# Attention backward on one Trainium2 core: fp32 transposes of X in two pairs inside the bank of transposed E, and six of E's transposes moved to DMA

## Chip, core and metric

The kernel runs on one core of one Trainium2 chip. The metric is the device time of one execution in microseconds. Three runs of the kernel before took 2244.68, 2246.61 and 2248.53 us; their median is 2246.61 us.

## What is computed

The reference is a forward pass and its gradients for a gated block over x of 2048 rows by 512 columns: `x + s * g`, where s is attention of the normalised x (32 heads of 16 columns) and g a gate made by an MLP of width 1792. Cut to what matters here:

```python
def _A_ref(x, wqkv, wo):
    qkv = (x @ wqkv).reshape(B, S, 3, H, Dh) ...
    scores = jnp.einsum("bhqd,bhkd->bhqk", q, k) * (Dh ** -0.5)
    p = _softmax(scores, axis=-1)
    o = jnp.einsum("bhqk,bhkd->bhqd", p, v)
    return o ... @ wo
...
_out, _vjp = jax.vjp(_f, A_x, A_wqkv, A_wo, B_w1, B_b1, B_w2, B_b2)
_grads = _vjp(grad_out)
```

The change lies in the attention, where output, dQ, dK and dV of each head are made.

## The kernel before, in words

The program has three parts: a preparation (layer norms, projections, MLP forward, gate), the attention core (function `attention_core`, from about 222 to about 1890 us of the span) and the remaining gradients. Only the attention core is touched.

**Blocks and steps.** The attention runs over 64 blocks: 16 pairs of heads times 4 groups of 512 queries. A block has 16 units, one for each 128 keys, kb = 0 to 15. The loop variable is the step g; unit g belongs to block g // 16 and has kb = g % 16. Below, "step 2" is the step with g % 16 = 2, and "unit 7" the unit with kb = 7. The work of the units is software-pipelined by hand, and the order on every engine is that in which the loop body issues it (no scheduler reorders it). In step g:

- TensorE (PE) makes `d` of unit g (dO times V, L1104, one bank of 512 columns for each of the two heads), the scores `s` of unit g + 1 (L1082), the transposes `tT` of unit g - 1 (L1166), three groups of products of unit g - 1 that are added into the block's bank `X` (L1196, L1199, L1203), and four products `Z` (L1280) of the block 20 steps back.
- ScalarE (ACT) takes the exponential of unit g + 1 into the ring `ets` (L1091), and then copies transposed blocks of unit g - 1 from PSUM to the tile `ek` in SBUF (L1178).
- VectorE (DVE) multiplies `d` by E for both heads of unit g into `gts` (L1121). Between the two it copies the share of the transposed blocks that ACT does not take (list `VCOPY`: 0, 1 or 2 of 7). Further copies come in single steps: `xs` from X in step 0 (L1212), `xt` from XT and a reciprocal in step 2 (L1234, L1244), and the sum `acc` from Z in steps 3 and 11 (L1292, L1294).
- SyncE's queue (SP) issues DMA transposes: `gk` from `gts`, 16 blocks of 128 by 128, after each odd unit (L1137); and `ekd` from `ets`, the one block in eight of E that TensorE does not transpose, 4 or 8 blocks at a time, in steps 4, 6, 12 or 14 (L1147, L1151, L1153).
- GpSimd (POOL) computes small factors from `xt` after step 2 and issues loads for the next pair of heads.

**The ring of E.** `ets` has three slots of four units. Unit kb of chunk c (four units a chunk) writes the quarter kb % 4 of slot c % 3, so the exponential of units 12 to 15 overwrites what units 0 to 3 of the same block left. An exponential waits for every reader of what it overwrites, DMA transposes included.

**PSUM.** Eight banks: two for `s`, one for `tT` (seven blocks of 128 by 128 in bf16), three that rotate among the `d`, one for X, one for Z. In step 2 of the next block, four fp32 transposes of `xs` (`XT`, L1222) take one of the three rotating banks; DVE copies it whole to `xt`, and the factors of the softmax and dQ and O follow from it.

Of the kernel before, what the change touches and what calls it, by code (L numbers as in the profile page):

```python
# [8 lines left out]
bf16 = mybir.dt.bfloat16  # L9
f32 = mybir.dt.float32  # L10
ACT = mybir.ActivationFunctionType
ALU = mybir.AluOpType
# [1005 lines left out]
def attention_core(ctx, ctx_r, tc, k, grads, Oall, dQall, dKVT_out, ident_f32, ident_bf, npairs=16, nqc=4):  # L1018
    nc = tc.nc
# [3 lines left out]
    ps_t = ctx.enter_context(tc.tile_pool(name="ps_t", bufs=1, space=PSUM, reuse_waits="tile"))  # L1023
    ps_d = ctx.enter_context(tc.tile_pool(name="ps_d", bufs=3, space=PSUM, reuse_waits="tile"))
# [8 lines left out]
    xsp = sb("xsp", 1)  # L1033
    finp = sb("finp", 1)
# [6 lines left out]
    ets = etp.tile([128, 3, 4, 2, 4, 128], bf16, name="ets")  # L1041
# [44 lines left out]
    def emit_exp(g):  # L1086

        a = a_unit(g)
        if a is None:
            return  # L1090
        nc.scalar.activation(out=st_et[g][:, :, :, a[1] % 4, :].rearrange("k b h q -> k h b q"),  # L1091
                             in_=cur["s"][:].rearrange("k h (b q) -> k h b q", b=4), func=ACT.Exp)
# [17 lines left out]
    def emit_mult(g):  # L1110
        a = a_unit(g)
        if a is None:
            emit_cT(g - 1, 7 - VCOPY[(g - 1) % 16], 7, nc.vector.tensor_copy)
            return
        kb = a[1]
        if kb % 2 == 0:
            cur["gts"] = gtp.tile([128, 2, 2, 512], bf16, name="gts")
        gts = cur["gts"]
        st_gt[g] = gts
        for hj in range(2):  # L1120
            nc.vector.tensor_tensor(out=gts[:, kb % 2, hj, :].rearrange("k (b q) -> k b q", b=4),  # L1121
                                    in0=st_d.pop((g, hj))[:].rearrange("k (b q) -> k b q", b=4),
                                    in1=st_et[g][:, :, hj, kb % 4, :], op=ALU.mult)
            if hj == 0:
                emit_cT(g - 1, 7 - VCOPY[(g - 1) % 16], 7, nc.vector.tensor_copy)

    def emit_dmat(g):
        a = a_unit(g)
# [19 lines left out]
        if kb % 8 == 6:  # L1148
# [3 lines left out]
            else:  # L1152
                nc.sync.dma_start_transpose(out=ek[:].rearrange("q c a k -> q (c a) k"),  # L1153
                                            in_=ets[:].rearrange("k s b h a q -> k (s b h) (a q)")[:, 8 * sl - 1:8 * sl + 1]
                                            .rearrange("k x q -> k (x q)"))

    def emit_T(g):
        a = a_unit(g)
        if a is None:
            return  # L1160
        kk = a[1] % 4
        et = st_et[g]
        t = ps_t.tile([128, 7, 128], bf16, name="tT")
        for i in range(7):
            b = i + a[1] // 4 % 2
            nc.tensor.transpose(t[:, i, :], et[:, b // 2, b % 2, kk, :], ident_bf[:])  # L1166
        st_T[g] = t
        if kk == 0:
            cur["ek"] = ekc.tile([128, 4, 7, 128], bf16, name="ek")
            blk[a[0]]["Ek"][a[1] // 4] = cur["ek"]  # L1170

    def emit_cT(g, lo, hi, copy):

        a = a_unit(g)
        if a is None or lo == hi:
            return
        j, kb = a
        copy(out=blk[j]["Ek"][kb // 4][:, kb % 4, lo:hi].rearrange("q i k -> q (i k)").bitcast(f32),  # L1178
             in_=st_T[g][:, lo:hi].rearrange("q i k -> q (i k)").bitcast(f32))

    def emit_x(g, part):
        a = a_unit(g)
# [23 lines left out]
    def emit_xs(g):  # L1206
# [5 lines left out]
        nc.vector.tensor_copy(out=xs[:], in_=blk[j].pop("X")[:])  # L1212
        blk[j]["xs"] = xs

    def emit_XT(g):
        j = g // 16 - 1
        if g % 16 != FIN_AT or not 0 <= j < NB:
            return
        xs = blk[j].pop("xs")
        XT = ps_d.tile([128, 4, 128], f32, name="XT", tag="d")  # L1220
        for qb in range(4):
            nc.tensor.transpose(XT[:, qb, :], xs[:, qb * 128:(qb + 1) * 128], ident_f32[:])  # L1222
        blk[j]["XT"] = XT

    def emit_fin(g):
        j = g // 16 - 1
        if g % 16 != FIN_AT or not 0 <= j < NB:
            return
        p, qc = blocks[j]
        NQq = k.op0["NATQq"]  # L1230
        NQd = k.op0["NATQd"]
        XT = blk[j].pop("XT")
        xt = xsp.tile([128, 4, 128], f32, name="xt", tag="xs")
        nc.vector.tensor_copy(out=xt[:], in_=XT[:])  # L1234
        xf = xt[:].rearrange("q b c -> q (b c)")
        XE = xf[:, 0:256].rearrange("q (b h c) -> q b h c", b=4, h=2)
        XG = xf[:, 256:512].rearrange("q (b h c) -> q b h c", b=4, h=2)
        W1, W2 = WT[j % 2]
        st0 = qc * 4
        nqs = NQq[:, st0:st0 + 4, :, :]  # L1240
        ndo = NQd[:, st0:st0 + 4, :, :]
        bc = lambda ap: ap.to_broadcast([128, 4, 2, 16])
        rL = finp.tile([128, 4, 2, 1], f32, name="rL")
        nc.vector.reciprocal(out=rL[:], in_=XG[:, :, :, 17:18])  # L1244
        nc.gpsimd.tensor_tensor(out=W2[:, :, :, 16:32], in0=nqs, in1=bc(rL[:]), op=ALU.mult)  # L1245
        ndl = finp.tile([128, 4, 2, 1], f32, name="ndl")
        nc.gpsimd.tensor_tensor(out=ndl[:], in0=XG[:, :, :, 0:1], in1=rL[:], op=ALU.mult)
        ndr = finp.tile([128, 4, 2, 1], f32, name="ndr")
        nc.gpsimd.tensor_tensor(out=ndr[:], in0=ndl[:], in1=rL[:], op=ALU.mult)
        nc.gpsimd.tensor_tensor(out=W1[:, :, :, 0:16], in0=ndo, in1=bc(rL[:]), op=ALU.mult)  # L1250
        nc.gpsimd.tensor_tensor(out=W1[:, :, :, 16:32], in0=nqs, in1=bc(ndr[:]), op=ALU.mult)
        Ov = Oall[:, st0:st0 + 4, p * 32:(p + 1) * 32].rearrange("q b (h c) -> q b h c", h=2)
        nc.gpsimd.tensor_tensor(out=Ov, in0=XE[:, :, :, 16:32], in1=bc(rL[:]), op=ALU.mult)
        t1 = finp.tile([128, 4, 2, 16], f32, name="t1")
        nc.gpsimd.tensor_tensor(out=t1[:], in0=XE[:, :, :, 0:16], in1=bc(ndl[:]), op=ALU.mult)
        nc.gpsimd.tensor_tensor(out=t1[:], in0=XG[:, :, :, 1:17], in1=t1[:], op=ALU.add)
        rL4 = finp.tile([128, 4, 2, 1], f32, name="rL4")
        nc.gpsimd.tensor_scalar(out=rL4[:], in0=rL[:], scalar1=0.25, scalar2=None, op0=ALU.mult)
        dQv = dQall[:, st0:st0 + 4, p * 32:(p + 1) * 32].rearrange("q b (h c) -> q b h c", h=2)
        nc.gpsimd.tensor_tensor(out=dQv, in0=t1[:], in1=bc(rL4[:]), op=ALU.mult)  # L1260

    def emit_z(g):
        u = z_unit(g)
# [39 lines left out]
    FIN_AT = 2  # L1303
# [5 lines left out]
    for g in range(NSTEP - ZOFF):  # L1309
        cur["g"] = g  # L1310
        a = a_unit(g)
        if a is not None:
            j, kb = a
            p, qc = blocks[j]
            if kb == 0 and qc == 0:
                L = natq_loads(k, k.op0, p, nc.gpsimd.dma_start) if p > 0 else []
                if p + 1 < npairs:
                    L += op_load_list(k, OP[(p + 1) % 2], p + 1, nc.gpsimd.dma_start)
                else:
                    L += grads.tail_loads(nc.gpsimd.dma_start)  # L1320
# [12 lines left out]
        emit_z(g + ZOFF)  # L1333
        emit_mult(g)
        emit_xs(g - 1)
        emit_fin(g)
        for it in [x for x in late if x[0] <= g]:
            late.remove(it)

            nc.gpsimd.tensor_copy(out=tick[:], in_=st_gt[g][0:1, kb % 2, 1, 510:512])  # L1340
            it[1]()
        emit_acc(g + ZOFF)
        if g >= NSTEP:
            grads.tail_mid(g - NSTEP)
        emit_cT(g - 1, 0, 7 - VCOPY[(g - 1) % 16], nc.scalar.copy)
        st_T.pop(g - 1, None)
        emit_dmat(g)
        st_gt.pop(g - 2, None)
        st_et.pop(g - 12, None)
        if g == NSTEP:  # L1350
            ctx_r.close()
            grads.tail_open(ps_t, ps_s, ps_d)
# [113 lines left out]
```

## Time and profile before

| what | before |
|---|---|
| median of three runs | 2246.61 us |
| profiled execution: span from first to last instruction | 2242.4 us |
| median of the runs less this span (what lies around it) | 4.2 us |
| mean granted TensorE clock | 0.991 |
| attention, 400 to 1600 us: PE, DVE, ACT busy | 1190.67, 1129.07, 1055.51 of 1200 us |
| attention, 400 to 1600 us: DMA | 200 GB/s |
| one block (start of the exponential of unit 0 to that of the next block's), median | 25.6 us |

A busy share on PE says little, since matmuls are pipelined and their ends are modelled. More is read from the distances between starts in the timeline: which row starts how long after which. On SP, an entry lasts from the moment the queue takes up a DMA until it can take up the next, so it holds the wait for the data and for room behind earlier transfers; the landing is a time of its own.

### The profile page before, as it was taken

The numbers are of one execution on the slowest core, as the hardware profiler recorded it, in microseconds if no ns is written. First come the engines' busy times: TensorE is split into PE (matmuls) and PEld (weight loads), VectorE is DVE, ScalarE is ACT, GpSimd is POOL, SyncE is SP. The second block draws the span as 40 slices with busy tenths as digits, with TensorE's granted clock in tenths as the row PEclk, the third lists the DMA queues.
The fourth block names the chain that finished last, engine by engine and source line by source line (L and its number), as shares of the span: only waits on it lengthen the run. The fifth ranks groups of instructions, "written<-read, shape, count | busy, mean of one in ns | idle before, by whom it ended". The sixth has DMA issues, their size and how long they took to land.

```text
span 2242.4 us, 74217 instructions
## 1 busy us (share of the span) xinstructions
PE 2160.1 (96%) x30690; PEld 1205.0 (54%) x30690; DVE 1912.2 (85%) x3626; ACT 1734.5 (77%) x2481; POOL 606.8 (27%) x1387
## 2 busy tenths in 40 slices
PE   6998999999999999999999999999999999989996
PEld 3444555555555555555555555555555554434443
DVE  6676799999999999999999999999999997777623
ACT  4764788888888888888888888888888886674213
POOL 4276413122222222131222222221312224310012
PEclk9999899999999999999999999999999999999998
DMA  7786999999999999999999999999999999899972
GB/s 238 242 273 197 184 199 194 202 200 203 195 203 194 200 197 206 196 199 200 198 203 197 203 192 204 199 199 197 204 196 190 204 205 273 194 257 240 233 222 94
DMA packets 1421747, 461.15 MB, mean 206 GB/s; under 512 B 1334622, under 2 KB 1405662, under 8 KB 1421408
## 3 DMA queue, kind: packets, MB, share of 16 engines
q1 hardware_dynamic: 1406880, 424.67, 99.3%
q0 software_dynamic: 12944, 30.16, 5.4%
q8 instruction: 240, 3.93, 0.8%
q10 hardware_dynamic: 1584, 1.57, 0.2%
q14 instruction: 99, 0.81, 0.1%
HBM read 62.79 MB, written 64.75 MB: 57 GB/s over the span
## 4 chain that ended last, share of the span: by engine, by line
PE 86%; DMA 5%; DVE 2%; issue 2%; ACT 2%; POOL 2%; SPq 0%; POOLq 0%; DVEq 0%; ACTq 0%
PE tT L1166 23%; PE d L1104 14%; PE X L1196 10%; PE Z L1280 10%; PE X L1199 5%; PE X L1203 5%; PE s L1082 2%; PE ps_m L367 2%; PE ps_dy L902 2%; PE ps_dw L973 2%; PE ps_dh L868 2%; PE ps_h L352 2%; DMA out_dram<-ot 2%; PE XT L1222 1%; PE ps_dwkv L820 1%
## 5 line engine op out<-in xcount | busy, mean ns | idle before, releaser
L1121 DVE TENSOR_TENSOR gts<-d,ets 128x512 bf16<-128x512 f32 x2048 | 1363.2, 684 | 101.0 <-ACT ek L1178 20.3
L1091 ACT ACTIVATE ets<-s 128x1024 bf16<-128x1024 f32 x1024 | 1048.7, 1024 | 198.5 <-PE s L1082 95.2
L1166 PE MATMUL tT<-ident_bf,ets 128*128 128x128 bf16 x7168 | 568.9, 219 | 16.7 <-ACT ek L1178 6.9
L1166 PEld LDWEIGHTS <-ets 128*128 128x128 bf16 x7168 | 445.5, 97 | 242.0 <-issue 240.2
L1178 ACT COPY ek<-tT 128x448 f32<-128x448 f32 (+2 forms) x1024 | 501.6, 490 | 8.1 <-DVE ek L1178 6.9
L1104 PE MATMUL d<-QDT,KVT 32*128 32x512 bf16 x2048 | 458.6, 385 | 0.0
L1082 PE MATMUL s<-QDT,KVT 32*128 32x512 bf16 x2048 | 401.6, 381 | 3.4 <-ACT ets L1091 3.2
L1104 PEld LDWEIGHTS <-KVT 32*128 32x128 bf16 x2048 | 145.4, 91 | 323.9 <-issue 323.9
L1196 PE MATMUL X<-ets,NAT 128*32 128x256 bf16 x4096 | 300.6, 284 | 0.1
L1203 PE MATMUL X<-gts,NAT 128*17 128x256 bf16 x4096 | 290.0, 273 | 0.0
L1199 PE MATMUL X<-ets,Lc 128*32 128x256 bf16 x4096 | 289.9, 273 | 0.0
L1340 POOL COPY tick<-gts 1x2 bf16<-1x2 bf16 x205 | 36.2, 176 | 606.1 <-DVE gts L1121 606.1
L1280 PE MATMUL Z<-gk,W 128*32 128x512 bf16 x2048 | 197.8, 379 | 1.0 <-DVE acc L1294 1.0
L1280 PE MATMUL Z<-ek,W 128*32 128x512 bf16 x1792 | 198.6, 379 | 0.0
L1245 POOL TENSOR_TENSOR W<-NATQq,rL 128x128 bf16<-128x128 bf16 x64 | 25.4, 397 | 526.1 <-DVE rL L1244 443.3
L1196 PEld LDWEIGHTS <-NAT 128*32 128x32 bf16 x4096 | 106.2, 93 | 110.8 <-issue 11.4
L1082 PEld LDWEIGHTS <-KVT 32*128 32x128 bf16 x2048 | 139.0, 91 | 12.5 <-issue 9.5
L1178 DVE COPY ek<-tT 128x64 f32<-128x64 f32 (+1 forms) x576 | 132.4, 230 | 5.5 <-POOL KVT L50 4.2
L1280 PEld LDWEIGHTS <-W 128*32 128x32 bf16 x4096 | 109.7, 97 | 11.4 <-issue 1.5
L1199 PEld LDWEIGHTS <-Lc 128*32 128x32 bf16 x4096 | 107.9, 96 | 0.0
L1203 PEld LDWEIGHTS <-NAT 128*17 128x17 bf16 x4096 | 103.6, 92 | 3.1
L1280 PE MATMUL Z<-ekd,W 128*32 128x512 bf16 x256 | 97.0, 379 | 0.0
(244 smaller groups left out, 2339.3 us busy)
## 6 DMA issues: line engine op xcount, KB each, us to landing
gk<-gts SPq DMA_TRANSPOSE x512, 5.1
H1T_s<-h1r SPq DMA_DIRECT2D x28, 256.0 KB, 4.3
HGT_s<-hgT SPq DMA_DIRECT2D x8, 896.0 KB, 4.6
DH_s<-stg SPq DMA_DIRECT2D x12, 512.0 KB, 3.1
hch<-DH_s SPq DMA_DIRECT2D x12, 512.0 KB, 4.7
gp<-H1T_s SPq DMA_DIRECT2D x9, 512.0 KB, 5.4
out_dram<-ob_w POOLq DMA_DIRECT2D x36, 128.0 KB, 4.1
NAT_s<-NS SPq DMA_DIRECT2D x4, 1056.0 KB, 6.2
```

The source lines that it names most:

```text
L352: nc.tensor.matmul(ps[:], lhsT=w1_sb[:, ic, fc * 128:(fc + 1) * 128], rhs=yT[:, ic, g * 512:(g + 1) * 512], start=(ic == 0), stop=(ic == I ...
L367: nc.tensor.matmul(ps[:], lhsT=hgT[:, g % 2, fc, t4 * 128:(t4 + 1) * 128], rhs=w2_sb[:, fc, :], start=(fc == 0), stop=(fc == FC - 1))
L1082: nc.tensor.matmul(s[:, hj, :], lhsT=op["KVT"][r:r + 32, kb * 128:(kb + 1) * 128], rhs=op["QDT"][r:r + 32, qc * 512:(qc + 1) * 512], start ...
L1091: nc.scalar.activation(out=st_et[g][:, :, :, a[1] % 4, :].rearrange("k b h q -> k h b q"), in_=cur["s"][:].rearrange("k h (b q) -> k h b q ...
L1104: nc.tensor.matmul(d[:], lhsT=op["KVT"][r:r + 32, kb * 128:(kb + 1) * 128], rhs=op["QDT"][r:r + 32, qc * 512:(qc + 1) * 512], start=True, ...
L1121: nc.vector.tensor_tensor(out=gts[:, kb % 2, hj, :].rearrange("k (b q) -> k b q", b=4), in0=st_d.pop((g, hj))[:].rearrange("k (b q) -> k b ...
L1166: nc.tensor.transpose(t[:, i, :], et[:, b // 2, b % 2, kk, :], ident_bf[:])
L1178: copy(out=blk[j]["Ek"][kb // 4][:, kb % 4, lo:hi].rearrange("q i k -> q (i k)").bitcast(f32), in_=st_T[g][:, lo:hi].rearrange("q i k -> q ...
L1196: nc.tensor.matmul(X[r:r + 32, 0:256], lhsT=NATt[:, kb, hj, 1:33], rhs=ev, start=(kb == 0), stop=False, skip_group_check=True, tile_positi ...
L1199: nc.tensor.matmul(X[r:r + 32, 256:512], lhsT=Lc[:], rhs=ev, start=False, stop=False, skip_group_check=True, tile_position=(0, r))
L1203: nc.tensor.matmul(X[r:r + 17, 256:512], lhsT=NATt[:, kb, hj, 0:17], rhs=gv, start=False, stop=(kb == 15), skip_group_check=True, tile_pos ...
L1280: nc.tensor.matmul(Z[r:r + 32, :], lhsT=WT[j % 2][1 - part][:, qb, hj, :], rhs=mv, start=(part == 0 and qb == 0), stop=(part == 1 and qb = ...
```

## The change

1. In units 1 and 2 of every block but the first, TensorE transposes four of the seven blocks (`cut` is 3), so the bank `tT` has its upper half free. ACT copies four blocks in place of seven there.
2. The four fp32 transposes of `xs` are made two at a time in steps 2 and 3, into that upper half of the bank of `tT`. They no longer take one of the rotating banks. DVE copies each half (256 columns) back over `xs`, between its two multiplications of the step (`emit_xt`), and POOL's small factors are divided between the two steps.
3. The three blocks of units 1 and 2 that are no longer transposed on TensorE are moved by three DMA transposes a block (`emit_Edma`), of 128 by 256 elements each, issued on SP in steps 4, 6 and 8 out of `ets` and into the same tile `ek`. Each stands in the queue ahead of what the step issues otherwise: in step 4 ahead of the `ekd` of that step if there is one, in step 6 ahead of `ekd`, in step 8 behind `gk` of unit 7. The exponential of unit 13 waits for the landing of all three.

In the order of the built program, SP has 189 more DMA transposes (3 in each of 63 blocks), and PE 378 fewer transposes (6 in each of 63 blocks). The exponential of unit 12 still waits for one `ekd`; that of unit 13, which waited for no DMA, waits for three. The copy of ACT in steps 2 and 3 now waits for DVE's copy of the half of XT.

```diff
@@ emit_mult
+            emit_xt(g)
...
             if hj == 0:
                 emit_cT(g - 1, 7 - VCOPY[(g - 1) % 16], 7, nc.vector.tensor_copy)
+                emit_xt(g)
@@
+    def cut(g):
+        return 3 if g >= 16 and g % 16 in (1, 2) else 0
+
+    def emit_Edma(g):
+        a = a_unit(g)
+        if a is None or a[0] == 0 or a[1] not in (4, 6, 8):
+            return
+        i = a[1] // 2 - 2
+        nc.sync.dma_start_transpose(out=blk[a[0]]["Ek"][0][:, 1:3, i, :],
+                                    in_=ets[:, (g - a[1]) // 4 % 3, i // 2, i % 2, 1:3, :].rearrange("k a q -> k (a q)"))
@@ emit_T
-        t = ps_t.tile([128, 7, 128], bf16, name="tT")
-        for i in range(7):
+        t = ps_t.tile([128, 512], f32, name="tT")
+        tb = t[:].bitcast(bf16).rearrange("q (i k) -> q i k", k=128)
+        for i in range(cut(g), 7):
             b = i + a[1] // 4 % 2
-            nc.tensor.transpose(t[:, i, :], et[:, b // 2, b % 2, kk, :], ident_bf[:])
+            nc.tensor.transpose(tb[:, i - cut(g), :], et[:, b // 2, b % 2, kk, :], ident_bf[:])
@@ emit_cT
+        c = cut(g)
+        lo = max(lo, c)
         copy(out=blk[j]["Ek"][kb // 4][:, kb % 4, lo:hi].rearrange("q i k -> q (i k)").bitcast(f32),
-             in_=st_T[g][:, lo:hi].rearrange("q i k -> q (i k)").bitcast(f32))
+             in_=st_T[g][:, (lo - c) * 64:(hi - c) * 64])
@@ emit_XT, emit_xt, emit_fin
+    def fin_half(g):
+        j = g // 16 - 1
+        if not 0 <= j < NB or g % 16 not in (FIN_AT, FIN_AT + 1):
+            return None
+        return j, (1, 0)[g % 16 - FIN_AT]
...
-        XT = ps_d.tile([128, 4, 128], f32, name="XT", tag="d")
-        for qb in range(4):
-            nc.tensor.transpose(XT[:, qb, :], xs[:, qb * 128:(qb + 1) * 128], ident_f32[:])
+        t = st_T[g - 1] if a_unit(g - 1) is not None else ps_d.tile([128, 512], f32, name="XT", tag="d")
+        XT = t[:, 256:512].rearrange("q (b c) -> q b c", b=2)
+        for b in range(2):
+            qb = 2 * h + b
+            nc.tensor.transpose(XT[:, b, :], xs[:, qb * 128:(qb + 1) * 128], ident_f32[:])
...
+        nc.vector.tensor_copy(out=blk[j]["xs"][:, 256 * h:256 * h + 256], in_=blk[j].pop("XT"))
...
-        nc.vector.tensor_copy(out=xt[:], in_=XT[:])
@@ the loop over steps
         emit_cT(g - 1, 0, 7 - VCOPY[(g - 1) % 16], nc.scalar.copy)
+        emit_Edma(g)
         st_T.pop(g - 1, None)
         emit_dmat(g)
```

More of the change, by code (lines that the diff above doesn't have):

```diff
@@ L1213, in emit_xs, with emit_xt @@
         blk[j]["xs"] = xs
+    def fin_half(g):
[3 more added lines that the diff above has]
+        return j, (1, 0)[g % 16 - FIN_AT]
     def emit_XT(g):
-        j = g // 16 - 1
-        if g % 16 != FIN_AT or not 0 <= j < NB:
+        f = fin_half(g)
+        if f is None:
             return
-        xs = blk[j].pop("xs")
-        XT = ps_d.tile([128, 4, 128], f32, name="XT", tag="d")
-        for qb in range(4):
-            nc.tensor.transpose(XT[:, qb, :], xs[:, qb * 128:(qb + 1) * 128], ident_f32[:])
-        blk[j]["XT"] = XT
+        j, h = f
+        xs = blk[j]["xs"]
+        t = st_T[g - 1] if a_unit(g - 1) is not None else ps_d.tile([128, 512], f32, name="XT", tag="d")
[3 more added lines that the diff above has]
+            nc.tensor.transpose(XT[:, b, :], xs[:, qb * 128:(qb + 1) * 128], ident_f32[:])
+        blk[j]["XT"] = t[:, 256:512]
+    def emit_xt(g):
+        f = fin_half(g)
+        if f is None:
+            return
+        j, h = f
+        nc.vector.tensor_copy(out=blk[j]["xs"][:, 256 * h:256 * h + 256], in_=blk[j].pop("XT"))
     def emit_fin(g):
-        j = g // 16 - 1
-        if g % 16 != FIN_AT or not 0 <= j < NB:
+        f = fin_half(g)
+        if f is None:
             return
+        j, half = f
         p, qc = blocks[j]
@@ L1231, in emit_fin @@
         NQd = k.op0["NATQd"]
[L1232 to L1235, printed above, removed]
+        xf = blk[j]["xs"][:]
         XE = xf[:, 0:256].rearrange("q (b h c) -> q b h c", b=4, h=2)
@@ L1242, in emit_fin @@
         bc = lambda ap: ap.to_broadcast([128, 4, 2, 16])
[L1243 to L1251, printed above, removed]
+        if half == 1:
+            rL = finp.tile([128, 4, 2, 1], f32, name="rL")
+            nc.vector.reciprocal(out=rL[:], in_=XG[:, :, :, 17:18])
+            nc.gpsimd.tensor_tensor(out=W2[:, :, :, 16:32], in0=nqs, in1=bc(rL[:]), op=ALU.mult)
+            ndl = finp.tile([128, 4, 2, 1], f32, name="ndl")
+            nc.gpsimd.tensor_tensor(out=ndl[:], in0=XG[:, :, :, 0:1], in1=rL[:], op=ALU.mult)
+            ndr = finp.tile([128, 4, 2, 1], f32, name="ndr")
+            nc.gpsimd.tensor_tensor(out=ndr[:], in0=ndl[:], in1=rL[:], op=ALU.mult)
+            nc.gpsimd.tensor_tensor(out=W1[:, :, :, 0:16], in0=ndo, in1=bc(rL[:]), op=ALU.mult)
+            nc.gpsimd.tensor_tensor(out=W1[:, :, :, 16:32], in0=nqs, in1=bc(ndr[:]), op=ALU.mult)
+            blk[j]["r"] = rL, ndl
+            return
+        rL, ndl = blk[j].pop("r")
         Ov = Oall[:, st0:st0 + 4, p * 32:(p + 1) * 32].rearrange("q b (h c) -> q b h c", h=2)
@@ L1260, in emit_fin @@
         nc.gpsimd.tensor_tensor(out=dQv, in0=t1[:], in1=bc(rL4[:]), op=ALU.mult)
+        blk[j].pop("xs")
     def emit_z(g):
```

## The prediction

> **What bounds the kernel now.** I read the page first (busy shares, chain, groups), then the timeline of one ordinary block, then the queue of SP. From the page:
>
> ```profile
> PE 2160.1 (96%) x30690; PEld 1205.0 (54%) x30690; DVE 1912.2 (85%) x3626; ACT 1734.5 (77%) x2481; POOL 606.8 (27%) x1387
> ...
> PE tT L1166 23%; PE d L1104 14%; PE X L1196 10%; PE Z L1280 10%; PE X L1199 5%; PE X L1203 5%; PE s L1082 2%; PE ps_m L367 2%; PE ps_dy L902 2%; PE ps_dw L973 2%; PE ps_dh L868 2%; PE ps_h L352 2%; DMA out_dram<-ot 2%; PE XT L1222 1%; PE ps_dwkv L820 1%
> ```
>
> The chain runs along PE, with the E transposes its largest part. In the timeline, PE rows of steps 1 and 2 of a block:
>
> ```profile
> 1000.65 0.55 PE L1166 MATMUL tT<-ident_bf,ets 128*128 128x128 bf16 x7
> 1001.16 0.29 PE L1196 MATMUL X<-ets,NAT 128*32 128x256 bf16 x4
> ...
> 1002.21 0.55 PE L1166 MATMUL tT<-ident_bf,ets 128*128 128x128 bf16 x7
> 1002.60 0.61 PE L1222 MATMUL XT<-ident_f,xs 128*128 128x128 f32 x4
> 1003.14 0.29 PE L1196 MATMUL X<-ets,NAT 128*32 128x256 bf16 x4
> ```
>
> Seven transposes occupy 1002.60 - 1002.21 = 0.39 us, 0.056 each. From tT to X it takes 0.51 us without XT and 0.93 with it, so XT costs PE 0.42. From start to start of the exponentials, an ordinary step takes 1.56 us, the one with XT 1.98, a block 25.6 (medians of the trace).
>
> ACT and DVE are close behind. Groups by form:
>
> ```profile
> L1178 ACT COPY ek<-tT 128x448 f32<-128x448 f32 x448 | 235.8, 526 | 0.6 <-PE tT L1166 0.6
> L1178 ACT COPY ek<-tT 128x384 f32<-128x384 f32 x448 | 212.1, 473 | 7.0 <-DVE ek L1178 6.5
> ...
> L1178 DVE COPY ek<-tT 128x64 f32<-128x64 f32 x448 | 96.4, 215 | 5.5 <-POOL KVT L50 4.2 <-PE tT L1166 0.4
> ...
> L1178 DVE COPY ek<-tT 128x128 f32<-128x128 f32 x128 | 36.0, 281 | 0.0
> ```
>
> An exponential (1.02) and a copy of 448 (0.53) make 1.55 of 1.56 us. DVE, from the copy of X in step 0 on:
>
> ```profile
> 1000.42 0.68 DVE L1212 COPY xs<-X 128x512 f32<-128x512 f32 x1
> 1001.02 2.56 DVE L1121 TENSOR_TENSOR gts<-d,ets 128x512 bf16<-128x512 f32 x4
> 1003.50 0.68 DVE L1234 COPY xt<-XT 128x512 f32<-128x512 f32 x1
> ...
> 1005.50 0.68 DVE L1292 COPY acc<-Z 128x512 f32<-128x512 f32 x1
> 1006.10 2.03 DVE L1121 TENSOR_TENSOR gts<-d,ets 128x512 bf16<-128x512 f32 x3
> ```
>
> Each row begins where the last ends: DVE has no pause through step 4.
>
> Last, SP, which no share on the page shows: the rows of `ekd`, then one block's rows on SP and ACT:
>
> ```profile
> L1153 SPq DMA_TRANSPOSE ekd<-ets x85: 1261/1268/2767, 239.9 to 1860.2; - x85
> L1147 SPq DMA_TRANSPOSE ekd<-ets x43: 1208/1212/2046, 250.1 to 1869.5; - x43
> ...
>   ACT ets L1091: 6.6, 11
> ...
> DMA to landing us min/median/max: 2.3/3.4/6.0
> ```
>
> ```profile
> 1010.63 1.35 SPq L1153 DMA_TRANSPOSE ekd<-ets  x1
> 1012.35 4.28 SPq L1137 DMA_TRANSPOSE gk<-gts  x1
> ```
>
> ```profile
> 1017.37 1.02 ACT L1091 ACTIVATE ets<-s 128x1024 bf16<-128x1024 f32 x1 [0.51 <-DMA ekd<-ets]
> ```
>
> Three things are to be seen. An `ekd` of 4 blocks holds SP for 1.21 us and one of 8 for 1.27: nearly all of it is independent of size. The `gk` entries (minimum 1.58, median 2.27, mean 2.42 us) stand end to end with `ekd`; their sum, 1239 us, and that of `ekd`, 225 us, make 1464 of the 1649 us that the core lasts. And the exponential of unit 12 (1017.37) waits 0.51 us for an `ekd` issued 6.7 us earlier. That happens 11 times: transposes that read the ring are already just in time.
>
> **The change, part by part** (63 blocks).
>
> *PE.* Six E transposes go: 6 x 0.056 = 0.33 us a block. The four of XT stay (0.42), as 0.21 in each of steps 2 and 3. Splitting could cost a start and a drain twice; but one XT starts 0.109 after another, and 4 x 0.109 is all of the 0.42, so I take nothing for it.
>
> *ACT.* Two copies shrink from 448 to 256 columns. One block of 64 fewer is worth 0.053 (526 to 473), so 0.16 each, 0.32 a block. It goes on top of PE's gain only as far as ACT's copy, not PE, holds the next transposes.
>
> *DVE.* One copy of 0.68 becomes two of 256 columns: (281 - 215) / 64 = 1.03 ns a column, so 0.215 + 192 x 1.03 = 0.41 each, 0.82 together, plus 0.14 at most; with the 0.08 by which DVE's entries overlap each other, about 0.07. Since DVE has no pause in steps 0 to 4, it can't follow PE's 0.33: what is late next is the second `d` of step 5, whose bank is freed by the first multiplication of step 4. ACT's copies in steps 2 and 3 now also stand behind DVE's half of XT, about 0.1 us each. That multiplication ends at 1006.10 + 0.68 = 1006.78; the `d` stands at 1006.96 and can come forward to 1006.83, 0.05 behind its releaser; the E transposes follow a `d` by 0.32 where nothing holds them (step 3: 1003.81 to 1004.13), so they start at 1007.15 and not, held by ACT's copy, at 1007.37. That is 0.22 to 0.23 us a block; bounds 0 and 0.53 (0.33, and both copies' gain beyond what PE gives). 63 x 0.23 = 14 us.
>
> *The rotating bank* that XT gives back is worth nothing beyond this: in the rows, no `d` waits for it. *POOL's split* costs nothing: Z needs the first factors only in step 4, the others in step 8.
>
> *SP.* Three transposes of 2 blocks each. The trace has none of this size. Nearest is the 4-block row, 1.21 us; in proportion to size it would be 0.60; flat, as 4 against 8 blocks shows, 1.2. I take 1.2, and 1.3 with the 0.09 between entries: 3.9 us of SP a block. The Trainium skill ("DMA: Bandwidth & Descriptors", Rules for kernel authors) says that under 64 KB a transfer pays mostly overhead, and each of these is 128 x 256 x 2 bytes, 64 KB; the flat 1.21 and 1.27 agree with it.
>
> Who waits? Not Z, which reads `ek` 16 steps later, but whoever overwrites the ring: the exponential of unit 13. Behind it on ACT are the copy for TensorE's next transposes and the next exponential, and PE's next `s` waits for the bank that it reads; between an exponential's end (1000.72 + 1.02) and that `s` (1001.82) lie 0.08 us, so what unit 13 waits, the block pays.
>
> From the end of SP's `gk` of unit 7 to the start of the exponential of unit 13 is 2.86 us (median of 62 blocks; the middle half 2.54 to 3.31). The third transpose starts 0.09 after that `gk` and lands 3.44 after its start (row above: 2.3 to 6.0): 3.53 - 2.86 = 0.67 us late, with nothing else moved. But the first two also stand ahead of that `gk`: 2.6 us less the 0.7 that SP idles before the `gk` of unit 5, so up to 1.9 more. Part of it vanishes, since a `gk` of 2.8 us against a minimum of 1.58 is mostly waiting behind earlier transfers. Between 0 and 1.9 I take 0.75. Wait of unit 13: 1.4 us. Unit 12 waits too, as its `ekd` comes up to 1.9 later: 0.1 to 0.2.
>
> *Sum.* 1.4 + 0.13 - 0.23 = 1.3 us a block, 63 x 1.3 = 82 us; less about 4 for SP catching up in the longer blocks: 78. On the profiled span, 2242.4 + 78 = 2320; the runs' median lies 4.2 above the span: **2325 us**, 3.5% slower.
>
> **Rivals.**
>
> *The landings are hidden (faster).* The mechanism is PE's shorter path. It decides the sign if the third transpose lands within 2.9 + 0.23 us of the `gk` entry's end: a 2-block transpose holds SP well under 1 us and lands near the minimum of 2.3. Then 0.09 + 2.3 - 2.86 is below zero, and 2246.6 - 14 = 2232 us. For it: smaller transfers, the `gk` entries hold 8 x (2.42 - 1.58) = 6.7 us a block over their minimum that could give way. Against it: the flat cost from 8 to 4 blocks, and the 11 waits. The Trainium skill (same page and section) says that a DMA issued early and waited for late has its fixed cost overlapped; the 0.51 us row disagrees, as the one who waits is the overwriter. 13%.
>
> *A draw*, waits of about 0.23 us: 2247. 5%.
>
> *SP becomes the bound.* If `gk` keeps its mean, a block needs 8 x 2.42 + 2.67 x 1.32 + 3 x 1.2 + 13.7 x 0.09 = 27.7 us of SP, 2.1 more than 25.6: 63 x 2.1 = 132, so 2378 us. Then `gk` entries fall ever further behind their `gts`, and multiplications wait for buffers. For it: SP's 89% (1464 of 1649). Against it: the `gk` minimum of 1.58. 17%, up to 2400.
>
> *The forecast*, waits of unit 13 that leave 2260 to 2360: 65%.
>
> **From these to the numbers.** Of the cases, 13% are faster than before by over 0.2% (4.5 us, about what a measurement can tell), 5% within, 82% slower. The range must reach from the hidden case's upper edge (2240, a tenth below) into the SP-bound one (2385, a tenth above).
>
> **What would show it.** Right: exponentials (L1091) waiting for DMA `ek<-ets`, about once a block, over 1 us; the step before unit 13 over 2.5 us; SP entries of about 1.2 us at the new line; from tT to X about 0.56 us in steps 2 and 3 (0.51 - 0.17 + 0.21) in place of 0.93 and 0.51. Wrong: new entries of 0.6 us, or no such waits; `gts` waiting for `gk` landings instead (SP bound); PE waiting for DVE in steps 2 to 5 for more than 0.33 us.

## The result, and the profile after

The changed kernel takes 2450.17 us (median; 2447.34 to 2462.1) beside 2245.64 us for the kernel before in the same rounds: a ratio of 1.0918, 95% interval 1.0897 to 1.094. It is slower by some 204 us. The forecast was 2325 us with a range up to 2385: the direction holds, the size does not.

The page of the changed kernel, its first line and its chain of work:

```profile
PE 2237.4 (91%) x30312; PEld 1202.6 (49%) x30312; DVE 1914.6 (78%) x3690; ACT 1737.7 (71%) x2481; POOL 605.0 (25%) x1387
...
PE 73%; DMA 9%; ACT 6%; DVE 5%; issue 4%; POOL 1%; SPq 1%; ACTq 0%; POOLq 0%; DVEq 0%
```

TensorE (PE) issues 378 fewer matmuls and yet is busy 77 us longer (2160.1 before): the same work has become slower in places. The mean granted clock of the profiled execution says so too, 0.954 after 0.991. The chain, which ran along PE, now lies 9% on DMA. What ScalarE (ACT) waits for, the lines of the exponential (us in total, times, longest):

```profile
ACT ets L1091 <- DMA ek<-ets: 88.5, 32, 5.3
...
ACT ets L1091 <- DMA ekd<-ets: 24.9, 24, 2.6
```

Such sums miss every wait that is put down to another semaphore, so I measured instead from start to start of the exponentials, over the 62 blocks with both a block ahead and one behind. A block lasts 25.69 us before and 28.98 after in the mean, 3.28 us more; 63 of these are 207 us, and the two profiled spans differ by 204.4. It divides so:

| distance between starts of exponentials | before, us | after, us | difference |
|---|---|---|---|
| steps 2 to 6 together | 8.32 | 8.09 | -0.23 |
| unit 11 to unit 12 | 1.61 | 1.89 | +0.27 |
| unit 12 to unit 13 | 1.56 | 3.90 | +2.34 |
| the next three (13 to 16) | 4.74 | 5.70 | +0.95 |
| all others | 9.45 | 9.40 | -0.05 |

**The gain is there.** Rows of PE in step 2 of a block of the changed kernel:

```profile
1009.93 0.38 PE L1180 MATMUL tT<-ident_bf,ets 128*128 128x128 bf16 x4
1010.15 0.39 PE L1247 MATMUL tT<-ident_f,xs 128*128 128x128 f32 x2
1010.47 0.29 PE L1212 MATMUL X<-ets,NAT 128*32 128x256 bf16 x4
```

From tT to X it takes 0.54 us in steps 2 and 3 (0.56 forecast, 0.92 and 0.50 before; medians).

**The wait of unit 13.** SP's queue in the same block, each row with its start and how long it holds the queue:

```profile
1015.04 1.20 SPq L1167 DMA_TRANSPOSE ek<-ets  x1
1016.43 2.01 SPq L1139 DMA_TRANSPOSE gk<-gts  x1
1018.49 1.24 SPq L1167 DMA_TRANSPOSE ek<-ets  x1
1019.82 1.26 SPq L1155 DMA_TRANSPOSE ekd<-ets  x1
1021.17 2.26 SPq L1139 DMA_TRANSPOSE gk<-gts  x1
1023.48 1.24 SPq L1167 DMA_TRANSPOSE ek<-ets  x1
```

Six entries end to end, three of them new. The trace has the landing of the last at 1027.02, 3.53 us after its start. ACT:

```profile
1025.20 0.53 ACT L1194 COPY ek<-tT 128x448 f32<-128x448 f32 x1
1027.16 1.02 ACT L1091 ACTIVATE ets<-s 128x1024 bf16<-128x1024 f32 x1 [1.44 <-PE tT L1180]
```

In the kernel before, unit 13 starts without a wait:

```profile
1018.93 1.02 ACT L1091 ACTIVATE ets<-s 128x1024 bf16<-128x1024 f32 x1
```

In the changed kernel it starts 0.14 us behind that landing, 1.44 us late. The releaser in the bracket is wrong here: the tT that it names was long done, and the transfer is the one thing found that ends at the right moment. This is how a DMA wait hides in the table of waits.

**The clock.** A longer wait, in another block (unit 13 starts at 1168.50, after 3.91 us of waiting). Stretches of 3.41 us, with busy time of PE, PEld, DVE, ACT and POOL, then the granted clock (PEclk), DMA share and GB/s:

```profile
1160.71:1164.13 3.42, 3.42 (x66) 1.80 (x54) 3.20 (x7) 3.04 (x6) 0.71 (x2) 1.00 0.63 140
1164.13:1167.54 3.41, 2.01 (x32) 1.06 (x29) 2.06 (x4) 0.46 (x2) 2.18 (x5) 1.00 1.23 174
1167.54:1170.95 3.41, 1.38 (x10) 0.76 (x9) 0.69 (x1) 2.12 (x3) 0.15 (x1) 0.50 1.11 133
1170.95:1174.37 3.42, 3.42 (x44) 1.66 (x43) 2.21 (x5) 2.29 (x4) 0.00 (x0) 0.50 1.27 286
1174.37:1177.78 3.41, 3.41 (x66) 1.85 (x58) 2.67 (x6) 2.55 (x5) 0.68 (x2) 1.00 0.74 165
```

The wait begins late in the second stretch, in which PE is busy for 2.01 of 3.41 us. In the third and fourth stretches TensorE's clock is at half, and in the fourth it does 44 matmuls where the first, as busy, holds 66. The kernel before, over the end of a block:

```profile
1017.37:1027.00 9.63, 9.54 (x163) 5.44 (x162) 8.76 (x17) 8.74 (x13) 1.33 (x4) 1.00 1.26 219
```

The half clock appears in 35 of the 62 blocks (177 us at half clock); the kernel before has none in its 62 blocks. Blocks with such a stretch spend 6.42 us in the three steps after unit 13, the others 4.76.

### The profile page after: what moved, and what is told of

It is laid out like the page before. It is cut to its first block, busy times and chain, and to the rows that moved or that the text cites. A ratio compares the mean times of both kernels' runs of the same rounds, so it can differ in the third digit from the quotient of the medians.

```text
span 2446.8 us, 73900 instructions
## 1 busy us (share of the span) xinstructions
PE 2237.4 (91%) x30312; PEld 1202.6 (49%) x30312; DVE 1914.6 (78%) x3690; ACT 1737.7 (71%) x2481; POOL 605.0 (25%) x1387
## 4 chain that ended last, share of the span: by engine, by line
PE 73%; DMA 9%; ACT 6%; DVE 5%; issue 4%; POOL 1%; SPq 1%; ACTq 0%; POOLq 0%; DVEq 0%
PE tT L1180 18%; PE d L1104 12%; PE X L1212 8%; PE Z L1315 8%; DMA ek<-ets 6%; ACT ets L1091 4%; PE X L1215 4%; PE X L1219 4%; PE s L1082 3%; DVE gts L1122 3%; PE ps_dy L902 2%; PE ps_m L367 2%; PE ps_dw L728 2%; PE ps_dw L973 2%; PE ps_dh L868 2%
## 5 line engine op out<-in xcount | busy, mean ns | idle before, releaser
L1180 PEld LDWEIGHTS <-ets 128*128 128x128 bf16 x6790 | 432.2, 100 | 264.2 <-issue 262.6
L1082 PE MATMUL s<-QDT,KVT 32*128 32x512 bf16 x2048 | 415.8, 395 | 139.2 <-ACT ets L1091 139.1
L1104 PE MATMUL d<-QDT,KVT 32*128 32x512 bf16 x2048 | 507.1, 397 | 0.0
L1194 ACT COPY ek<-tT 128x384 f32<-128x384 f32 (+3 forms) x1024 | 483.3, 472 | 10.2 <-DVE ek L1194 5.1
L1104 PEld LDWEIGHTS <-KVT 32*128 32x128 bf16 x2048 | 148.5, 91 | 336.4 <-issue 336.4
L1212 PE MATMUL X<-ets,NAT 128*32 128x256 bf16 x4096 | 307.0, 290 | 0.4 <-DVE xs L1228 0.3
L1215 PE MATMUL X<-ets,Lc 128*32 128x256 bf16 x4096 | 297.7, 281 | 0.0
L1219 PE MATMUL X<-gts,NAT 128*17 128x256 bf16 x4096 | 297.6, 281 | 0.0
L1082 PEld LDWEIGHTS <-KVT 32*128 32x128 bf16 x2048 | 142.5, 91 | 169.7 <-issue 166.6
L1315 PE MATMUL Z<-gk,W 128*32 128x512 bf16 x2048 | 211.6, 406 | 1.1 <-DVE acc L1329 1.1
L1315 PEld LDWEIGHTS <-W 128*32 128x32 bf16 x4096 | 116.4, 99 | 14.9 <-issue 1.8
```

Source lines behind the costliest of these rows:

```text
L1082: nc.tensor.matmul(s[:, hj, :], lhsT=op["KVT"][r:r + 32, kb * 128:(kb + 1) * 128], rhs=op["QDT"][r:r + 32, qc * 512:(qc + 1) * 512], start ...
L1104: nc.tensor.matmul(d[:], lhsT=op["KVT"][r:r + 32, kb * 128:(kb + 1) * 128], rhs=op["QDT"][r:r + 32, qc * 512:(qc + 1) * 512], start=True, ...
L1180: nc.tensor.transpose(tb[:, i - cut(g), :], et[:, b // 2, b % 2, kk, :], ident_bf[:])
L1212: nc.tensor.matmul(X[r:r + 32, 0:256], lhsT=NATt[:, kb, hj, 1:33], rhs=ev, start=(kb == 0), stop=False, skip_group_check=True, tile_positi ...
L1215: nc.tensor.matmul(X[r:r + 32, 256:512], lhsT=Lc[:], rhs=ev, start=False, stop=False, skip_group_check=True, tile_position=(0, r))
L1219: nc.tensor.matmul(X[r:r + 17, 256:512], lhsT=NATt[:, kb, hj, 0:17], rhs=gv, start=False, stop=(kb == 15), skip_group_check=True, tile_pos ...
```

## Experiments

**Theory A:** the whole loss comes from the three transposes: each holds SP 1.2 us whatever its size, pushes what stands behind it, and the exponentials that overwrite the ring wait for landings; the long waits then drop the clock. **Rival B:** it comes from the shared PSUM bank and the copies that now wait for each other. **Rival E** (in a form of its own below, **G**): not the deadline that the ring sets for the new transposes but SP's total is the bound. In the tables, times are in us, and a wait is the mean distance from one exponential to the next above 1.56 us.

### The two halves of the change

Only the PSUM side (`cut_only`; the blocks that no DMA moves are zeroed), and only the DMAs (`dma_only`; `emit_Edma` as in the changed kernel):

```diff
--- after, cut_only
-        emit_Edma(g)
+                nc.gpsimd.memset(cur["ek"][:, 1:3, 0:3, :], 0.0)   # kb == 0
--- before, dma_only
...
+        emit_Edma(g)
```

> The changed kernel without its three DMA transposes a block. Leaves out: the six blocks of transposed E a block that these moved (blocks 0 to 2 of units 1 and 2) are zeroed once by GpSimd, so these products of Z are made of zeros. Theory A (the whole loss hangs on the three landings: the exponential of unit 13 waits for them, and TensorE's clock falls after the long waits): about 14 us under the kernel before, 2232 us, from the 0.23 us a block that steps 2 to 6 gain; the step of unit 13 back at 1.56 us, no half-clock stretches. Rival B (the loss comes from the PSUM side: the transposes of X in the bank of E's transposes, copies of DVE and ACT that now wait for each other): still well over the kernel before, above 2300 us. Zeroing costs GpSimd up to 1 us a block beside other work; if it shows, it is in steps 0 and 1.

> The kernel before with the three DMA transposes a block added and nothing else (TensorE still makes these blocks too, and the DMA writes the same values over them). Theory A (the landings are the whole loss): the changed kernel's time plus the 14 us that the shorter TensorE path gained, about 2465 us; the step of unit 13 near 3.9 us in the mean, half-clock stretches in about half of the blocks. Rival B (the PSUM side makes the loss): near the kernel before, 2246 to 2270 us.

Measured: `cut_only` 2241.78 us, ratio 0.9987 (0.9967 to 1.0007); `dma_only` 2475.01 us, ratio 1.1013 (1.0992 to 1.1034). B falls: the DMAs alone lose more than the whole change, and the PSUM side alone loses nothing. But it hardly gains either: 5 us in the median where 14 were expected, and the interval takes in no gain at all. Its steps 2 to 6 do gain 0.20 us a block; unit 12 then waits 0.13 us longer than before (0.18 against 0.05), probably because a shorter block gives SP less time (not tested by itself), and in 3 of the 62 blocks that wait drops the clock as well. So the change could hardly have won more than 0.3% (the interval's lower end) with DMAs that cost nothing.

### Which entry costs what

One or two of the three entries, and all three in other steps:

```diff
--- after, third_only (two_only: "not in (4, 6)"; blocks that no DMA moves are zeroed)
-        if a is None or a[0] == 0 or a[1] not in (4, 6, 8):
+        if a is None or a[0] == 0 or a[1] != 8:
--- after, early
-        if a is None or a[0] == 0 or a[1] not in (4, 6, 8):
+        if a is None or a[0] == 0 or a[1] not in (2, 3, 4):
-        i = a[1] // 2 - 2
+        i = a[1] - 2
```

> The changed kernel with the third DMA transpose alone (step 8, behind gk of unit 7). Leaves out: the four blocks of transposed E a block that the first two moved are zeroed by GpSimd. Theory A (the wait of unit 13 is the landing of the third against the ring's deadline, and the first two add to it by standing ahead in the queue): without them the third starts about 3.6 us after the multiplication of unit 7 in place of 5.3, so unit 13 waits 0.7 to 1.0 us in the mean in place of 2.34; waits over 2.5 us, and with them half-clock stretches, in few blocks; 2280 to 2300 us. Rival D (the third is late by itself, whatever stands ahead): the wait stays above 1.8 us and the time above 2350 us.

> The changed kernel with the first two DMA transposes alone (steps 4 and 6). Leaves out: the two blocks of transposed E a block that the third moved are zeroed by GpSimd. Theory A: unit 13 waits for nothing, since both land some 5 us ahead of it; gk of unit 7 still starts some 3 us after its multiplication (0.8 before), ekd about 2.3 us later than before, so unit 12 waits 0.2 to 0.4 us in the mean; 2240 to 2265 us. Rival E (SP's total is what costs, so each entry costs a third of the loss): about 2246 - 14 + 2/3 x 218 = 2377 us.

> The changed kernel with its three DMA transposes issued in steps 2, 3 and 4 in place of 4, 6 and 8. Theory A1 (the place in the queue is what costs: the third lands after the deadline that the ring sets at unit 13): the third starts some 4 to 6 us sooner, unit 13 waits little, and the time is 2235 to 2270 us, with few or no half-clock stretches. Rival A2 (SP's total of the block is what costs: three entries of 1.2 us push everything behind them wherever they stand): the loss only moves, to the multiplications that wait for landings of gk or to the exponential of unit 12 that waits for its ekd, and the time stays above 2350 us.

| kernel | us | unit 12 waits | unit 13 waits | gk of unit 7 starts late by | SP: entries + rest = block | blocks at half clock |
|---|---|---|---|---|---|---|
| before | 2246 | 0.05 | 0.00 | 0.82 | 22.82 + 2.87 = 25.69 | 0 |
| third_only | 2317 | 0.11 | 1.15 | 0.93 | 23.58 + 3.47 = 27.05 | 17 |
| two_only | 2328 | 0.80 | 0.02 | 3.81 | 25.15 + 1.91 = 27.06 | 19 |
| early | 2404 | 1.60 | 0.04 | 4.72 | 26.28 + 1.90 = 28.18 | 23 |
| after | 2450 | 0.33 | 2.34 | 3.24 | 25.23 + 3.75 = 28.98 | 35 |

`third_only`: the wait halves, so the first two do push the third; but 2317 is above the 2280 to 2300 expected, and its 1.15 us above the upper end. Its two runs took 2304 and 2331 us, and the trace is that of the longer one, so the sizes in this row are the least certain of the table. `two_only` was expected at 2240 to 2265 by theory A and at 2377 by rival E; 2328 fits neither. `early` takes the wait from unit 13 entirely, and unit 12 gets 1.60 us of it, for the `ekd` that now stands behind three entries: 2404, on the side of A2.

The sixth column tells part of why. The rest of a block beside SP's entries is of two kinds: about 0.09 us from one entry to the next, and time in which SP has nothing to issue. The second kind can be seen because an entry does not hold the wait for its data, other than the section on the time and profile before says: in these traces no `gk` entry starts before its multiplication has ended. In `early` and `two_only` the rest is 1.9 us, of which gaps under 0.2 us make 1.1, so SP is nearly full. But SP's sum alone does not set the length of a block. In 39 of the 62 blocks of either kernel some `gk` starts within 0.1 us of its multiplication, so SP has caught up there. Its lateness grows over a block or two, and then an exponential pays for it in one long wait, after which the clock often falls: the blocks with a half-clock stretch last 29.74 us in `two_only` and 30.71 in `early`, the others 25.87 and 26.69. In the changed kernel the rest is 3.75 us, and the wait of unit 13 lets SP catch up in 61 of 62 blocks (`gk` of unit 1 is 0.40 us late, against 1.3 in `early` and `two_only`).

### SP's queue without the new deadline

The same three entries in the same steps, reading a tile that nothing overwrites:

```diff
--- after, static_src
-                                    in_=ets[:, (g - a[1]) // 4 % 3, i // 2, i % 2, 1:3, :].rearrange("k a q -> k (a q)"))
+                                    in_=op_of(a[0])["QDT"][:, 256 * i:256 * i + 256])
```

> The changed kernel with its three DMA transposes reading from a tile that nothing overwrites meanwhile (QDT, the transposed operands of the pair) in place of the ring of E. Leaves out: the six blocks of transposed E a block, in whose place stand transposes of QDT. So no exponential waits for the three, and all that is left is what their entries cost on SP. Theory G (two limits stand one behind the other: without the ring's deadline SP's queue itself is the bound, as in the kernels with two entries, with one of 12 blocks and with early ones, whose blocks last as long as SP's entries plus 1.9 us): backlog is no longer caught up from block to block, unit 12 waits for its ekd by 1 to 2 us in the mean, a block lasts 28.0 to 28.4 us, 2390 to 2420 us. Rival A (the ring's deadline of unit 13 is the cause, and without it SP has room): unit 12 waits 0.2 to 0.4 us as in the changed kernel, 2250 to 2270 us.

Measured: 2383.39 us, ratio 1.0609 (1.0551 to 1.0667); a block lasts 27.94 us, of which SP's entries are 26.24, and the rest is 1.71. Of the transfers, ACT's exponentials now wait for the old ones only:

```profile
ACT ets L1091 <- DMA ekd<-ets: 96.6, 52, 4.4
```

A, in its narrow form that the deadline of unit 13 is all, falls: it would have given 2250 to 2270 us. G comes close in size, just under its 28.0 us, its 2390 us and its 1 to 2 us for unit 12 (0.95). Its picture is only half right, though: SP does catch up, in 22 of the 62 blocks. The loss is paid at deadlines that the ring had set for `ekd` all along: unit 12 waits for it 28 times by more than 0.3 us (64 us in all) and unit 4 19 times (31 us), since `ekd` now comes later, and 28 blocks have a half-clock stretch (30.07 us a block, the others 26.19). Against `cut_only`, the three entries cost 142 us though nothing overwrites their source; the deadline of unit 13 adds the last 67. Both figures hold the price of the clock. So A's chain of causes stands (entries push, an exponential waits to overwrite the ring, the clock drops), with more than one place where the wait can come up.

### One entry in place of three

```diff
--- after, merged
-        return 3 if g >= 16 and g % 16 in (1, 2) else 0
+        return 3 if g >= 16 and g % 16 < 4 else 0
-        if a is None or a[0] == 0 or a[1] not in (4, 6, 8):
+        if a is None or a[0] == 0 or a[1] != 4:
...
+        nc.sync.dma_start_transpose(out=blk[a[0]]["Ek"][0][:, 0:3].rearrange("q i a k -> q (i a) k"),
+                                    in_=ets[:, (g - a[1]) // 4 % 3].rearrange("k b h a q -> k (b h a q)")[:, 0:1536])
```

> One DMA transpose of 12 blocks a block in step 4 in place of three of 2 blocks: blocks 0 to 2 of units 0 to 3 (which lie side by side in the ring) are moved, so units 0 and 3 also lose three transposes on TensorE each, and the tile ek is laid out by block first. Theory A (an entry holds SP about as long whatever its size, so one entry of 1.3 to 1.5 us takes the place of 3.9, pushes what stands behind it by no more than that, and lands ahead of the deadline): unit 13 waits for nothing, unit 12 waits 0.2 to 0.3 us in the mean for its ekd, steps 2 to 6 gain 0.23 us or a little more; 2235 to 2255 us. Rival F (an entry is paid by its blocks, so 12 blocks hold SP at least 3 us): ekd and gk come as late as in the changed kernel, unit 12 waits over 0.5 us, and the time is above 2280 us.

Measured: 2316.09 us, ratio 1.0325 (1.0298 to 1.0352). The new entries of this kernel, min/median/max in ns:

```profile
L1166 SPq DMA_TRANSPOSE ek<-ets x63: 1417/1496/3014, 262.8 to 1929.9; - x63
```

Twice the blocks of the changed kernel's three entries for 1.50 us of the queue in place of 3.7: on the entry itself the price is nearly flat, and F's 3 us fall. Not quite all of the size is free: the next `gk`, that of unit 5, takes 2.81 us in the mean here, 2.20 in the kernel before. Two thirds of the loss are gone. But the time misses the 2235 to 2255, and what F said of the rest came true: `gk` of unit 7 starts 3.2 us late, as in the changed kernel, unit 12 waits 0.79 us, not 0.2 to 0.3, and the time is above 2280. SP's rest is again 1.91 us a block, and 15 blocks fall to half clock. Even this one entry came to more than SP could take without delaying `ekd`. No form of the change that was run beats the kernel before.

### Whose time is the 1.2 us?

The three DMAs on ACT's queue (`nc.scalar` in place of `nc.sync` in `emit_Edma`):

> The changed kernel with its three DMA transposes issued on ScalarE's queue in place of SP's, at the same places of the program. Theory H (the 1.2 us of an entry are the issuing queue's own time): gk and ekd come as early as in the kernel before, unit 13 waits for nothing or little, but ScalarE, which has no pause, loses 1.2 us three times a block, 63 x 3.6 = 227 us, so 2440 to 2480 us. Rival I (the 1.2 us are room in the transfer rings that all queues share): gk entries grow by about as much as the entries that left, SP's lateness stays near 3 us. If ScalarE's part is short (0.1 us each), the time is 2240 to 2290 us.

Measured: 3081.02 us, ratio 1.3715 (1.3661 to 1.3768), outside both expectations. The entries on ACT's queue, and their landings:

```profile
L1167 ACTq EVENT_SEMAPHORE  x273: 17/38/6375, 261.4 to 2690.8; - x137
L1167 ACTq DMA_TRANSPOSE ek<-ets x189: 1183/1185/2035, 265.0 to 2699.0; - x189
...
DMA to landing us min/median/max: 2.3/2.3/3.2
```

In the trace each of these entries starts after the landing of SP's transpose ahead of it (in all 120 of 189 cases in which that landing is known), and SP's next entry only after its own landing (0.05 to 0.44 us after it); ACT waits up to 6.4 us for that, and every block is at half clock for a while. The order is the program's. The Trainium skill ("DMA: Bandwidth & Descriptors", Rules for kernel authors) asks that transposes of two queues be serialized. So the time tells nothing of H against I. The entry does: with no other transpose in flight, it still holds its queue 1.185 us. That is the price of issuing, not room behind earlier transfers, and H holds that far.

### What drops the clock

First, eight more matmuls of `d` in the wait (`busy`); then no transfers at all, but one, two or three repeats of the exponential of unit 13 in the kernel before (`stall1`, `stall`, `stall3`):

```diff
--- after, busy
+        if a is not None and a[0] > 0 and a[1] == 13:
+            for _ in range(8):
+                emit_d2(g, 0)
--- before, stall
         emit_exp(g + 1)
+        if a is not None and a[0] > 0 and a[1] == 12:
+            emit_exp(g + 1)
+            emit_exp(g + 1)
```

> The changed kernel with eight more matmuls of d (the same values written again to the same bank, about 1.7 us) on TensorE in the step in which it waits for the exponential of unit 13, ahead of the scores of unit 14. Theory C1 (the clock falls because TensorE stands idle in that wait): fewer half-clock stretches than 36 of 62 blocks, steps 13 to 15 near 1.6 us in place of 1.64, 2.13 and 1.93, so up to 0.9 us a block less, 57 us: 2395 to 2430 us, although blocks with a wait under 1.7 us lose some tenths. Rival C2 (the clock falls for another cause, such as the load of the transfers): the half-clock stretches stay, and the extra matmuls cost up to 0.3 us a block: 2450 to 2470 us.

Measured: 2475.44 us, ratio 1.1032 (1.1006 to 1.1058). Half-clock stretches in 27 blocks in place of 35 (133 us in place of 177), so C1's direction, but the time went the other way: the step of unit 13 grew to 4.12 us and the next to 1.98. In 20 of its 24 falls between 260 and 1860 us, a pause of 1.45 us or more was still left behind the extra matmuls. By itself it decides nothing.

> The kernel before, with no new transfers, in which ScalarE takes the exponential of unit 13 three times in place of once (the same values), in 63 blocks: 2 x 1.02 = 2.05 us in which TensorE waits, at the place and of the length of the wait in the changed kernel. Theory C1 (TensorE's clock falls to half for 3.4 us when a stretch of 3.4 us of a fixed grid was more than some 0.4 idle): half-clock stretches in over half of the blocks, steps 13 to 15 near 2 us in the mean; about 2246 + 63 x (2.05 + 0.9) = 2430 us. Rival C2 (the clock falls because of the transfers, not of the pause): no half-clock stretches in the blocks, 2246 + 63 x 2.05 = 2376 us.

> The kernel before with the exponential of unit 13 taken twice (one repeat, about 1.03 us more on ScalarE in each of 63 blocks). Theory C1, made sharper by the run with two repeats (there TensorE paused for 1.72 us; the clock fell wherever 1.59 us or more of the pause lay in one stretch of a fixed 3.41 us grid, and nowhere below 1.51): the pause here is about 0.7 us, under that in every block, so no half-clock stretch from it, and the cost is the wait alone: 2246 + 63 x 1.0 = 2309 us. Rival C3 (any pause may drop the clock, longer ones more often): half-clock stretches in about a quarter of the blocks, 2330 us.

> The kernel before with the exponential of unit 13 taken four times (three repeats, about 3.1 us more in each of 63 blocks). Theory C1: TensorE pauses for about 2.8 us, so in some 90 of 100 positions against the grid at least 1.6 us of it lie in one stretch: half-clock stretches in over 50 of 62 blocks, each costing some 1.5 us; 2246 + 63 x 3.1 + 55 x 1.5 = 2524 us. Rival C3 (about half of the blocks, as with two repeats, the position having nothing to do with it): 2246 + 195 + 46 = 2487 us.

| kernel | us | TensorE's pause | blocks of 62 at half clock | step of unit 13 | the next two steps |
|---|---|---|---|---|---|
| before | 2246 | - | 0 | 1.60 | 3.14 |
| stall1 | 2299 | 0.67 | 2 | 2.57 | 3.15 |
| stall | 2405 | 1.72 | 30 | 3.63 | 3.75 |
| stall3 | 2553 | 2.78 | 61 | 4.86 | 5.06 |

("Step of unit 13" here is from its first exponential to that of unit 14.) `stall` falls between C1's 2430 and C2's 2376, with half-clock stretches in 30 of 62 blocks where C1 said over half. C2 falls all the same: no transfer was added, and the clock drops. Two of its pauses, of the same length, in one answer:

```profile
893.56:896.97 3.41, 2.13 (x35) 1.27 (x35) 1.53 (x4) 3.11 (x6) 0.00 (x0) 1.00 1.15 138
896.97:900.38 3.41, 3.41 (x60) 1.96 (x57) 3.21 (x7) 3.13 (x5) 0.00 (x0) 1.00 0.90 199
948.17:951.58 3.41, 1.71 (x30) 0.99 (x29) 1.42 (x3) 3.32 (x5) 0.66 (x2) 1.00 1.14 137
951.58:955.00 3.42, 3.42 (x37) 1.81 (x34) 2.04 (x5) 2.04 (x4) 0.00 (x0) 0.50 0.75 170
```

Where PE was busy for 2.13 of the 3.41 us, the next stretch keeps the full clock; where it was busy for 1.71, the next runs at half. All half-clock stretches of one run begin on one grid: their starts, modulo 3413.33 ns, agree within about 2 ns. In `stall`, 29 of the 30 falls come after a grid stretch that held 1.59 us or more of the pause, and the 32 blocks without a fall had at most 1.51. With `stall1` next to none falls and with `stall3` nearly every block, as C1 said and C3 did not. The threshold is less sharp than `stall` alone makes it. In `stall3`, five falls came after a stretch that held only 1.23 to 1.38 us of the pause, its first part, while in the one block without a fall the second part, 1.58 us, was not enough. So it lies somewhere between 1.2 and 1.6 us of 3.41, and may depend on which end of the stretch the pause lies at. `stall3` costs more than C1's 2524, since most of its falls (55 of 61) last two stretches. The changed kernel agrees: its 29 falls between 260 and 1860 us follow grid stretches in which PE was busy for at most 62% of the time, in the median 39%. The Trainium skill ("TensorE: Matmul & The Clock Gate", section HAM oscillation) gives as its rule to avoid idle gaps of TensorE over about 3.4 us. In this case's traces half of that was enough (1.72 us).

## Why the prediction was wrong, step by step

- **PE, ACT and DVE: -0.23 us a block.** Right in kind and size: steps 2 to 6 are shorter by 0.23. That DVE, without a pause, keeps the rest also fits: the step that held XT is 0.35 us shorter, and step 6 gives 0.13 of it back. The 14 us that I made of it did not come through even without the DMAs: `cut_only` gains 5 us, not clear of the noise, as unit 12's longer wait takes 0.13 us a block back. Neither the rotating bank nor POOL's split was tried by itself; in `cut_only`, which has both, nothing else shows.
- **The entries: 1.2 us flat.** Right for these: 1.167/1.239/2.337 us (min/median/max), and 1.50 for six times the blocks.
- **Who waits.** Right: the exponential of unit 13, once a block, most of them over 1 us; unit 12 by 0.27 us more, where 0.13 was taken.
- **The push, 0.75 of 0 to 1.9.** This term failed. SP's `gk` of unit 7 ends 3.53 us after its multiplication in `third_only` and 5.34 in the changed kernel (medians): a push of 1.8, at the upper end. I let the `gk` entries give way to the new ones; the `gk` of unit 7 gave 0.5 us (2.84 to 2.35), all eight 0.2 in the mean. In unit 13's wait the push is 2.34 - 1.15 = 1.19 us.
- **0.67 us late with nothing moved.** Too low as well: `third_only`, which is this case, waits 1.15. I subtracted medians (3.53 - 2.86), with the landing of `ekd` for that of the new entry; in `third_only` they land 3.9 us after their start in the mean, and a wait that cannot go below nothing has a mean above the difference of medians. Together the wait is 2.34 and not 1.4 us.
- **What follows a wait.** This is the other step that failed: I priced a wait at its own length and what comes after it at nothing. The steps behind it lose 0.95 us more a block, which no step of the forecast has: the clock. 35 blocks of 62, 1.66 us each (6.42 - 4.76), are 58 us; the longer wait of unit 13 is 59 us (63 x 0.94), that of unit 12 about 9. With the 4 us that I took off for SP catching up, these make 130 us, beside the 125 between 2325 and 2450: about half is the mis-sized wait, about half the clock. The 27 blocks without a half-clock stretch last 27.01 us, 1.32 more than before, which is the 1.3 that I forecast; but they are the ones with the shorter waits, so this is no confirmation.
- **The rivals.** "SP becomes the bound" at 2378 us was not the outcome, though `static_src`, with the new deadline gone, stands at 2383. That the two numbers agree is in part luck: the rival had `gk` falling ever further behind and multiplications waiting for buffers, while in `static_src` SP catches up in 22 blocks, exponentials wait for `ekd` (96.6 us against 24.9 us that multiplications wait for `gk`), and the clock adds its part. What holds is that I had SP's fullness as an alternative to the waits, where it makes the waits and keeps them from being moved away. "Hidden landings" was out by any route that was run: it needed entries well under 1 us, and the least was 1.167.

What stays open: why SP's entries of `gk` take 2.0 to 2.4 us against a minimum of 1.58 (in `act_q`, where transposes often follow a landing, those of units 5 to 11 take 1.60 to 1.64 in the median, which speaks for room behind earlier transfers but was not tested by itself), and where exactly the threshold of the clock lies between 1.2 and 1.6 us. A ring with a fourth slot, which would move the deadlines, was not tried.

## What to carry to other kernels

Work that moved from a busy engine to DMA transposes was paid here by the entry far more than by the byte: before moving such work, add up the queue's entries over one period, and if they come near the period (here 22.8 of 25.7 us), an added entry delays the transfers behind it, and whoever reads or overwrites in time for them pays. Look for that deadline at the one who overwrites the source, and price it with the spread of landings, not with the median. And a pause of TensorE can cost more than its length: in this case those that lay within one 3.4 us stretch for some 1.2 to 1.6 us or more halved the clock.

## What the hardware showed that was not expected

- TensorE's clock is decided on a fixed 3.41 us grid: a pause of 1.72 us drops it or not by where it falls (it dropped in 30 blocks of 62); 0.67 us drops it hardly ever (2 of 62), 2.78 nearly always (61). A fall after 1.72 us cost 1.53 us a block in `stall` (28.97 against 27.45).
- A DMA transpose of 2 blocks and one of 12 differ by a fifth in what they take of the issuing queue (1.24 and 1.50 us, medians), and 1.185 us of it remain with no other transpose in flight.
